# Attention loop: batch preparation of K and V spread over turns, first additions on GpSimd, router sums for five tiles at once

## The chip, the cores and the metric

The kernel runs on one core of a Trainium2 chip. A core has five engines with an instruction queue each, which meet only through semaphores: TensorE (PE in the profile; its weight loads are PEld), VectorE (DVE), ScalarE (ACT), GpSimd (POOL) and SyncE (SP), which here only issues transfers. Data lie in SBUF (128 partitions) and in PSUM, where TensorE writes its products. The metric is device time in microseconds (us), lower is better.

## The reference

Three stages follow each other. First, attention over pooled keys and values: 8 batches, 8 heads, 576 positions, head size 64; each run of 8 positions of K and V is averaged, so a batch has 72 keys per head. Then a mixture of 8 experts, each token in its best two by noisy logits. Last, a dense layer of width 2048.

```python
k_p = k.reshape(B, H, Sp, pool, D).mean(axis=3)      # pool = 8, Sp = 72
v_p = v.reshape(B, H, Sp, pool, D).mean(axis=3)
scores = scale * np.matmul(q, k_p.transpose(0, 1, 3, 2))
scores = scores - np.max(scores, axis=-1, keepdims=True)
attn = np.exp(scores)
attn = attn / (np.sum(attn, axis=-1, keepdims=True) + 1e-09)
x = np.matmul(attn, v_p)                             # then to (4608, 512)
...
logits = x @ w_gate
noise_scale = np.log1p(np.exp(x @ w_noise))
noisy_logits = logits + noise_scale * noise          # two best experts of each token
...
h = np.maximum(x[mask] @ w1[e], 0.0)
out[mask] += top2_w[mask, k, None] * (h @ w2[e])     # for each expert
...
h = x @ w_in
g = h - np.tanh(h)
return (g @ w_out).astype(np.float32)
```

## The kernel before

The 4608 tokens are 36 tiles of 128. A batch is 4.5 tiles, so batch b begins in tile T0 = floor(4.5 b): 0, 4, 9, 13, 18, 22, 27, 31. The attention loop has 42 turns (`for t in range(NT + 6)`), and a tile goes through it as through a pipeline. Turn t issues for different tiles, in this order on each engine:

- TensorE: small products of the batch preparation (`pe_step`), the transposes of the weights of attention of tile t-2 (`st_attT`, L1330), of q of tile t+2 (`st_q`, L1288), the scores of tile t+1 (`st_scores`, L1298), the product with the router's weights of tile t-5 (`st_x`, L1355, into the one buffer px), and attention times V of tile t-3 (`st_av`, L1342).
- VectorE: the reciprocal of the sums of tile t-1 (`st_norm`, L1316 and L1319), reading px of tile t-6 (`st_g`: xr L1364, lg L1367, and the sum lz L1368), the two maxima of the scores of tile t+1 (mx, L1301), and then the jobs of the turn (`at_step`).
- ScalarE: exponentials (L1312) and the copies out of PSUM (xT L1348, aT L1331, qT L1290, kb L1278).

All engines run their queues strictly in this written order (`manual_schedule`), so a VectorE job that is long makes the next turn's lg late; TensorE's next product L1355 needs px, which lg frees, and everything behind L1355 waits as well.

The batch preparation, for each b: K and V are loaded with the eight positions of a pool side by side in a row, and three additions halve them (`add` with n = 4, 2 and 1: 128x1280, 128x640 and 128x320 elements). For K the result is spread with a mask (`ke`, L1233), transposed by TensorE (L1276) and copied by ScalarE (L1278) into `KB[b % 2]`; this is `kb`, at the head of turn T0-2. For V a maximum (`vm`, L1243) goes over TensorE and VectorE to a power of two (`vt`: L1247 and L1250; `vs`: L1254, then L101 to L1269), and `vs` writes `VB[b % 2]` (L1260). Each batch has two buffers for its K and V: kt_109 and vt_111 for even b, kt_110 and vt_112 for odd b. The jobs stand at fixed turns:

```python
at(max(T0 - 4, 0), add, nc.vector, b, "k", 4)
at(max(T0 - 3, 1), P[b]["k"])
at(max(T0 - 2, 1), add, nc.vector, b, "v", 4)
at(max(T0 - 1, 2), P[b]["v"])
at_pe(T0 - (1 if b == 1 else 2), P[b]["kb"])
```

Into the same turns go the preparation of the first expert's weights (`Prep`: four loads, four `amax` of 128x1024, four `high` on ScalarE, four `low` of 128x1024 on VectorE, for w1 and then w2), and for each group of some ten tiles the router's jobs (`gate_jobs`, then `lists`): from the turn in which the group's last lz is there, `tick()` puts about seven of their small VectorE instructions into each turn, between those above. `lists` has two instructions of 128x800 (l_one, l_col) and five of 128x256 (l_row) for each five tiles. After the loop come the experts and the dense layer, in which TensorE is busy nearly without a gap.

Of the kernel before, what the change touches and what calls it, by code (L numbers as in the profile page):

```python
# [10 lines left out]
F32 = mybir.dt.float32  # L11
# [4 lines left out]
OP = mybir.AluOpType  # L16
AX = mybir.AxisListType
# [1092 lines left out]
def attention(nc, tc, st, V):  # L1110
    q, k, v, w_gate, w_noise, noise = (V[n] for n in ("q", "k", "v", "w_gate", "w_noise", "noise"))
    B, H, S, D, N, E, DM, SP, NT, HP = (V[n] for n in ("B", "H", "S", "D", "N", "E", "DM", "SP", "NT", "HP"))
# [113 lines left out]
    def prep_jobs(b, first=False):  # L1226
        tl = {}

        def kpool():
            add(nc.vector, b, "k", 2)  # L1230
            add(nc.vector, b, "k", 1)
            tl["ke"] = wk.tile([128, 5, 2, D], F32, name="ke", bufs=1)
            tt(tl["ke"], KV[b, "k"][:, :, 0:1].to_broadcast([128, 5, 2, D]), odd[:, :, :, None].to_broadcast([128, 5, 2, D]),  # L1233
               op=OP.mult)

        def vpool():
            add(nc.vector, b, "v", 2)
            add(nc.vector, b, "v", 1)
            tl["va"] = KV[b, "v"]

        def vmax():
            tl["vm"] = wk.tile([128, 1], F32, name="vm")
            nc.vector.tensor_reduce(tl["vm"], tl["va"][:, :, 0], axis=AX.XY, op=OP.max, apply_absolute_value=True)  # L1243

        def vmaxT():
            p = ps.tile([1, 128], F32, name="pt", bufs=4)
            nc.tensor.transpose(p, tl["vm"], identf)  # L1247
            yield
            tl["vx"] = wk.tile([1, 1], F32, name="vx")
            nc.vector.tensor_reduce(tl["vx"], p, axis=AX.X, op=OP.max)  # L1250

        def vscale():
            p = ps.tile([128, 1], F32, name="pt", bufs=4)
            nc.tensor.matmul(p, ones1, tl["vx"], start=True, stop=True)  # L1254
            yield
            m = wk.tile([128, 3], F32, name="vs")
            pow2(nc, m, p)
            of8 = wk.tile([128, 5, 4], F32, name="of8")
            ts(of8, of, m[:, 2:3], None, op0=OP.mult)
            tt(VB[b % 2].rearrange("p c (j d) -> p c j d", d=D), tl["va"][:, :, 0:1].to_broadcast([128, 5, 4, D]),  # L1260
               of8[:, :, :, None].to_broadcast([128, 5, 4, D]), op=OP.mult)
            lo, hi = b * S, b * S + S
            t0, t1 = lo // 128, -(-hi // 128)
            for t in range(t0, t1):
                o0, o1 = max(lo - 128 * t, 0), min(hi - 128 * t, 128)
                if o1 - o0 < 128:
                    ts(isc[o0:o1, t:t + 1], m[o0:o1, 1:2], 1.0 / 128, None, op0=OP.mult)
            f0, f1 = -(-lo // 128), hi // 128
            ts(isc[:, f0:f1], m[:, 1:2].to_broadcast([128, f1 - f0]), 1.0 / 128, None, op0=OP.mult)  # L1269

        def kbd():
            for i, (c0, c1) in enumerate(((0, 3), (3, 5))):
                w = cuts[c1] - cuts[c1 - 1]
                p = ps.tile([128, 4, 128], F32, name="pt", bufs=4)[:, 0:c1 - c0, 0:w]
                for c in range(c0, c1):
                    nc.tensor.transpose(p[:, c - c0], tl["ke"][:w, c].rearrange("p i d -> p (i d)"), identf[:w, :w])  # L1276
                o = KB[b % 2][:, cuts[c0]:cuts[c1]].rearrange("p (c n) -> p c n", n=w)
                nc.scalar.activation(o, p, AF.Copy, scale=1.0 / 512)  # L1278
            yield
        return dict(k=kpool, v=vpool, vm=vmax, vt=vmaxT, vs=vscale, kb=kbd)  # L1280

    QT, SC, AT, ATT, PV, XT, SM, RC = {}, {}, {}, {}, {}, {}, {}, {}

# [71 lines left out]
            nc.tensor.matmul(p[:, m, 0:128 + 4 * E], xT[:, m], wgn[:, m], start=True, stop=True)  # L1355

    PX = {}

    def st_g(t):
        p, rc = PX.pop(t), RC.pop(t)  # L1360
        xr = wk.tile([128, DM], F32, name="xr", bufs=3)
        r = rc.rearrange("p (m i) -> p m i", i=2)[:, :, :, None]
        h = lambda a, n: a.rearrange("p m (i n) -> p m i n", n=n)
        tt(xr.rearrange("p (m i n) -> p m i n", m=HP, i=2), h(p[:, :, 0:128], D), r.to_broadcast([128, HP, 2, D]), op=OP.mult)  # L1364
        nc.sync.dma_start(x_d[128 * t:128 * t + 128, :], xr)
        lg = wk.tile([128, HP, 2, 2 * E], F32, name="lg", bufs=1)
        tt(lg, h(p[:, :, 128:128 + 4 * E], 2 * E), r.to_broadcast([128, HP, 2, 2 * E]), op=OP.mult)  # L1367
        nc.vector.tensor_reduce(lz[:, t], lg.rearrange("p m i e -> p e (m i)"), axis=AX.X, op=OP.add)  # L1368

    def psum(shape):  # L1370
        return ps.tile(shape, F32, name="pt", bufs=4)
# [137 lines left out]
    def at_pe(t, f):  # L1509
        pe_step.setdefault(t, []).append(f)  # L1510
        assert len(pe_step[t]) < 3

    P = {0: prep_jobs(0)}
    st_q(0)
    P[0]["k"]()
# [6 lines left out]
    at(0, P[0]["v"])  # L1522
    at(0, P[0]["vm"])
    at_pe(1, P[0]["vt"])
    at_pe(2, P[0]["vs"])
    TB = {b: (b * S) // 128 for b in range(B)}
    for b in range(1, B):
        P[b] = prep_jobs(b)
        T0 = TB[b]
        d = 1 if b == 1 else 0  # L1530
        if b > 1:
            at(T0 - 8, load_kv, b, "k")
            at(T0 - 7, load_kv, b, "v")
# [38 lines left out]
    for f, t in ((c1.fin1, 8), (c1.fin2, 12), (c2.fin1, 30), (c2.fin2, 33)):  # L1572
        at_pe(t, f)
    for j in range(4):
        at(1 + j, c1.load, [j])
        at(3 + j, c1.amax, j)
        at((12, 14, 15, 16)[j], c1.high, j, nc.scalar)
        at((13, 15, 16, 18)[j], c1.low, j)
        at(18 + 2 * j, c2.load, [j])
        at((21, 24, 26, 29)[j], c2.amax, j)  # L1580
# [102 lines left out]
```

## Time and profile before

| what | value |
|---|---|
| median of 3 runs | 1862.28 us (1858.55 to 1862.8) |
| profiled execution, first to last instruction | 1863.0 us |
| TensorE busy | 1775.1 us (95%) |
| VectorE busy | 1315.9 us (71%) |
| ScalarE busy | 940.7 us (50%) |
| GpSimd busy | 205.7 us (11%) |
| mean granted TensorE clock | 0.986 |

The profiled execution has no other time than its span, which lies 0.7 us above the median and 0.2 us above the slowest of the three runs. Shares of the whole span say little of the attention loop, which takes its first 250 us and has its own limits: its turns have to be read one by one in the timelines of TensorE and VectorE. A timeline's row names in brackets the idle time ahead of an instruction and what ended it. The granted clock is a share of 2.4 GHz: 0.5 is 1.2 GHz.

### The profile page before, as it was taken

How to read it: one execution, taken by the hardware profiler on the slowest of the kernel's cores; microseconds unless marked ns; L12 is line 12 of the kernel's file. 1: busy time of each engine (PE TensorE's matmuls, PEld its weight loads, DVE VectorE, ACT ScalarE, POOL GpSimd, SP SyncE). 2: the span in 40 equal slices, each digit the busy share in tenths (PEclk: the TensorE clock that was granted, in tenths of full speed). 3: DMA queues.
4: the chain of work that ended last, by engine and by line, in shares of the span. 5: the costliest groups of instructions: out<-in, count | busy, mean ns of one | idle time of the engine just before them, and what ended most of it. 6: DMA issues, size and time to landing. Idle time of an engine off the chain costs nothing. (4 is left out here: it accounts for less than half of the span.)

```text
span 1863.0 us, 28938 instructions
## 1 busy us (share of the span) xinstructions
PE 1775.1 (95%) x10791; PEld 1083.6 (58%) x10792; DVE 1315.9 (71%) x2680; ACT 940.7 (50%) x2249; POOL 205.7 (11%) x198
## 2 busy tenths in 40 slices
PE   7898889999999999999999999999999999999998
PEld 5887884444445454544545454566666666666664
DVE  5788877667666667666666456687878778787875
ACT  5686652343434344343434245565656666666554
POOL 1000000311203021110101012110100101010000
PEclk8898999999999999999999999999999999999999
DMA  9657323354474545453464344531313323141200
GB/s 217 186 156 209 86 75 108 108 160 119 138 223 117 160 136 157 135 158 88 139 155 118 88 122 117 119 86 33 91 41 68 77 45 84 30 91 42 40 24 25
DMA packets 264158, 203.45 MB, mean 109 GB/s; under 512 B 188160, under 2 KB 208640, under 8 KB 264000
## 3 DMA queue, kind: packets, MB, share of 16 engines
q1 hardware_dynamic: 251840, 162.16, 32.2%
q0 software_dynamic: 11904, 38.81, 8.1%
q8 instruction: 88, 1.44, 0.3%
q14 instruction: 70, 0.57, 0.1%
q10 hardware_dynamic: 256, 0.46, 0.1%
HBM read 121.82 MB, written 45.74 MB: 90 GB/s over the span
## 5 line engine op out<-in xcount | busy, mean ns | idle before, releaser
L359 ACT ACTIVATE hT<-ph 128x512 f16<-128x512 f32 (+2 forms) x192 | 96.8, 504 | 429.4 <-PE ph L357 429.2
L355 PE MATMUL ph<-xTp,pair 128*128 128x384 f16 (+2 forms) x736 | 247.1, 336 | 16.1 <-DVE hT L360 5.5
L356 PE MATMUL ph<-xTp,pair 128*128 128x384 f16 (+2 forms) x736 | 246.9, 335 | 0.4 <-DVE xTp L336 0.4
L357 PE MATMUL ph<-xTp,pair 128*128 128x384 f16 (+2 forms) x736 | 246.6, 335 | 0.0
L360 DVE SCALAR_TENSOR_TENSOR hT<-ph,hT 128x512 f16<-128x512 f32 (+2 forms) x192 | 110.6, 576 | 164.0 <-ACT hT L359 163.7
L1042 PE MATMUL py<-wo,gT 128*128 128x512 f16 x576 | 218.3, 379 | 1.0 <-DVE gT L989 1.0
L377 PE MATMUL py<-pair,hT 128*128 128x512 f16 x576 | 218.6, 379 | 0.0
L378 PE MATMUL py<-pair,hT 128*128 128x512 f16 x576 | 218.6, 379 | 0.0
L379 PE MATMUL py<-pair,hT 128*128 128x512 f16 x576 | 218.4, 379 | 0.0
L1040 PE MATMUL py<-wo,gT 128*128 128x512 f16 x576 | 218.3, 379 | 0.0
L1041 PE MATMUL py<-wo,gT 128*128 128x512 f16 x576 | 218.3, 379 | 0.0
L899 PEld LDWEIGHTS <-wi 128*128 128x128 f16 x1536 | 150.2, 98 | 71.3 <-issue 14.6
L315 POOL DMA_INDIRECT xg<-x_d,idx x75 | 85.3, 1138 | 676.5 <-DVE xp L342 467.9
L713 POOL DMA_INDIRECT y<-y_d,ridx x64 | 66.7, 1042 | 538.5 <-DVE y L724 238.4
L355 PEld LDWEIGHTS <-pair 128*128 128x128 f16 x768 | 75.4, 98 | 85.8 <-issue 27.8
L356 PEld LDWEIGHTS <-pair 128*128 128x128 f16 x768 | 75.4, 98 | 64.1 <-issue 9.0
L357 PEld LDWEIGHTS <-pair 128*128 128x128 f16 x768 | 75.6, 98 | 58.2 <-issue 2.6
L999 ACT ACTIVATE th<-th,bias 128x512 f32<-128x512 f32 x144 | 102.5, 712 | 3.3 <-DVE th L997 3.3
L1000 DVE SCALAR_TENSOR_TENSOR th<-th,t 128x512 f32<-128x512 f32 x144 | 98.4, 683 | 1.4 <-ACT th L999 1.4
L989 DVE TENSOR_TENSOR gT<-th,gT 128x512 f16<-128x512 f32 x144 | 98.6, 685 | 0.2 <-ACT gT L988 0.2
L1312 ACT ACTIVATE at<-psc,mx 128x72 f32<-128x72 f32 x288 | 87.5, 332 | 19.1 <-DVE mx L1301 19.1
L1042 PEld LDWEIGHTS <-gT 128*128 128x128 f16 x576 | 56.4, 98 | 69.3 <-DVE gT L989 1.4
(303 smaller groups left out, 3461.6 us busy)
## 6 DMA issues: line engine op xcount, KB each, us to landing
stage<-in_moe_w SPq DMA_DIRECT2D x64, 512.0 KB, 6.5
y_d<-ys SPq DMA_DIRECT2D x82, 256.0 KB, 2.1
x_d<-xr SPq DMA_DIRECT2D x36, 256.0 KB, 2.2
out<-o SPq DMA_DIRECT2D x36, 256.0 KB, 2.0
qt<-in_q SPq DMA_DIRECT2D x32, 256.0 KB, 6.3
raw<-in_moe_w_in SPq DMA_DIRECT2D x32, 256.0 KB, 3.0
raw<-in_moe_w_out SPq DMA_DIRECT2D x32, 256.0 KB, 3.1
kt<-in_k SPq DMA_DIRECT2D x7, 768.0 KB, 6.9
```

What stands on the lines that cost most here:

```text
L355: nc.tensor.matmul(p[:, :nt], w[:, 0, m, s], x[:, 0, m, :nt], start=(m == 0), stop=False)
L356: nc.tensor.matmul(p[:, :nt], w[:, 0, m, s], x[:, 1, m, :nt], start=False, stop=False)
L357: nc.tensor.matmul(p[:, :nt], w[:, 1, m, s], x[:, 0, m, :nt], start=False, stop=(m == KD - 1))
L360: stt(h[:, 1, :nt], p[:, :nt], 0.0, h[:, 0, :nt], op0=OP.max, op1=OP.subtract)
L377: nc.tensor.matmul(p, h[:, 0, s], w[:, 0, f], start=(f == 0), stop=False)
L378: nc.tensor.matmul(p, h[:, 0, s], w[:, 1, f], start=False, stop=False)
L379: nc.tensor.matmul(p, h[:, 1, s], w[:, 0, f], start=False, stop=(f == KF - 1))
L899: nc.tensor.matmul(p, w[:, a, m], y[:, c, b, m], start=(start and m + x == 0), stop=(m == 1 and x == 2), skip_group_check=True)
L999: nc.scalar.activation(q, q, AF.Square, bias=bias[:, 2:3], scale=SP5)
L1040: nc.tensor.matmul(p, g[:, 0, s], wo[:, 0, f], start=(f == 0), stop=False)
L1041: nc.tensor.matmul(p, g[:, 0, s], wo[:, 1, f], start=False, stop=False)
L1042: nc.tensor.matmul(p, g[:, 1, s], wo[:, 0, f], start=False, stop=(f == KF - 1))
```

## The change

It does five things. The first additions (n = 4) of K and V of batches 2 to 7 go from VectorE, where each was one instruction of 128x1280, to GpSimd, as five of 128x256. The remaining steps of K and V become single jobs (`k2`, `k1` with ke, `v2`, `v1` with vm), for which a small planner picks, in a window of turns ahead of the batch, the turn with the least load on its own list (`load`, in ns); ke is there two turns or more ahead of `kb`. `vt` and `vs` come one turn later (for b above 1), and V's load one turn later. The loads of the first expert's w1 go from turns 1 to 4 to turns 5 to 8, and its `amax`, `high` and `low`, like those of w2, to later turns, by the planner too. And lz is summed once for five tiles (four at two places, two at the end) out of a larger lg, in place of once for each tile.

```diff
-        def kpool():
+        def k2():
             add(nc.vector, b, "k", 2)
+
+        def k1():
             add(nc.vector, b, "k", 1)
             tl["ke"] = wk.tile([128, 5, 2, D], F32, name="ke", bufs=1)
...
+    sums = (0, 5, 10, 15, 20, 25, 29, 34)
...
-        lg = wk.tile([128, HP, 2, 2 * E], F32, name="lg", bufs=1)
-        tt(lg, h(p[:, :, 128:128 + 4 * E], 2 * E), r.to_broadcast([128, HP, 2, 2 * E]), op=OP.mult)
-        nc.vector.tensor_reduce(lz[:, t], lg.rearrange("p m i e -> p e (m i)"), axis=AX.X, op=OP.add)
+        if t in sums:
+            LG[0] = wk.tile([128, 5, HP, 2, 2 * E], F32, name="lg", bufs=2)
+            LG[1] = t
+        lg, t0 = LG
+        tt(lg[:, t - t0], h(p[:, :, 128:128 + 4 * E], 2 * E), r.to_broadcast([128, HP, 2, 2 * E]), op=OP.mult)
+        if t + 1 in sums or t + 1 == NT:
+            nc.vector.tensor_reduce(lz[:, t0:t + 1], lg[:, 0:t + 1 - t0].rearrange("p t m i e -> p t e (m i)"),
+                                    axis=AX.X, op=OP.add)
...
+    def first(b, nm):
+        for c in each:
+            add(nc.gpsimd, b, nm, 4, slice(*c))
+
+    for t in range(15, 35):
+        fixed(t, 1300)
...
-            at(T0 - 7, load_kv, b, "v")
-        at(max(T0 - 4, 0), add, nc.vector, b, "k", 4)
-        at(max(T0 - 3, 1), P[b]["k"])
-        at(max(T0 - 2, 1), add, nc.vector, b, "v", 4)
-        at(max(T0 - 1, 2), P[b]["v"])
-        at_pe(T0 - (1 if b == 1 else 2), P[b]["kb"])
-        at(T0 - 1 + d, P[b]["vm"])
-        at_pe(T0 + d, P[b]["vt"])
-        at_pe(T0 + 1 + d, P[b]["vs"])
...
+            at(T0 - 6, load_kv, b, "v")
+            at(T0 - 6, first, b, "k")
+            at(T0 - 4, first, b, "v")
+            chain((640, T0 - 5, T0 - 4, job["k2"]), (960, T0 - 5, T0 - 4, job["k1"]))
+            chain((640, T0 - 3, T0 - 1, job["v2"]), (640, T0 - 3, T0 - 1, job["v1"]))
+            at_pe(T0 - 2, job["kb"])
+        at_pe(T0 + 1, job["vt"])
+        at_pe(T0 + 2, job["vs"])
+        fixed(T0 + 2, 2000)
...
+    chain(*((1024, 8 + j, 9 + j, lambda j=j: c1.amax(j)) for j in range(4)))
+    chain(*((1024, 17 + j, 18 + j, lambda j=j: c1.low(j)) for j in range(4)))
...
-        at(1 + j, c1.load, [j])
+        at(5 + j, c1.load, [j])
...
+    for ops in sorted(spread, key=lambda ops: ops[0][2]):
+        t = 0
+        for w, lo, hi, f in ops:
+            t = min(range(max(lo, t), hi + 1), key=lambda t: load.get(t, 0))
+            fixed(t, w)
+            at(t, f)
```

What this makes of the order is seen at three places. First VectorE, before: turn 10 ends and turn 11 begins, with the jobs of turn 10 between: `vs` of batch 2 (vs to isc), and after it the second and third addition of batch 3's K and its ke, which `kb` at the head of turn 11 needs.

```order
L1301 TENSOR_REDUCE mx<-psc 128x4 x2
L101 TENSOR_SCALAR vs<-pt 128x1
L102 TENSOR_SCALAR vs<-vs 128x1
L103 TENSOR_SCALAR vs<-vs 128x1
L1259 TENSOR_SCALAR of_980<-of,vs 128x20
L1260 TENSOR_TENSOR vb_155<-vt_111,of_980 128x1280
L1267 TENSOR_SCALAR isc<-vs 64x1
L1269 TENSOR_SCALAR isc<-vs 128x4
L1141 TENSOR_TENSOR kt_110<-kt_110 128x5x128
L1141 TENSOR_TENSOR kt_110<-kt_110 128x5x64
L1233 TENSOR_TENSOR ke<-kt_110,odd 128x640
L1316 TENSOR_SCALAR sm<-sm 128x8
```

VectorE, after: the same additions and ke of batch 3 (line numbers are a few higher), now among the jobs of turn 9.

```order
L1303 TENSOR_REDUCE mx<-psc 128x4 x2
L1141 TENSOR_TENSOR kt_110<-kt_110 128x5x128
L1141 TENSOR_TENSOR kt_110<-kt_110 128x5x64
L1235 TENSOR_TENSOR ke<-kt_110,odd 128x640
L1318 TENSOR_SCALAR sm<-sm 128x8
L1321 RECIPROCAL rc<-sm 128x8
L1368 TENSOR_TENSOR xr<-px,rc 128x512
L1374 TENSOR_TENSOR lg<-px,rc 128x128
```

They have moved ahead by a turn and a half, and `vs` of batch 2, now in turn 11, has no other job in its turn.

The second place is SP's queue in turns 1 to 4, before: kt_109 and vt_111 are K and V of batch 2, stage takes w1, qt the q of a tile.

```order
L1135 DMA kt_109<-in_k 128x3x512
L1135 DMA kt_109<-in_k 96x2x512
L118 DMA stage<-in_moe_w 128x1024
L1157 DMA qt<-in_q 128x8x64
L1135 DMA vt_111<-in_v 128x3x512
L1135 DMA vt_111<-in_v 96x2x512
L1542 DMA nz<-in_moe_noise 128x36x8
L118 DMA stage<-in_moe_w 128x1024
L1157 DMA qt<-in_q 128x8x64
L118 DMA stage<-in_moe_w 128x1024
L1157 DMA qt<-in_q 128x8x64
L118 DMA stage<-in_moe_w 128x1024
```

SP's queue, after, from the second half of the same K load on.

```order
L1135 DMA kt_109<-in_k 96x2x512
L1157 DMA qt<-in_q 128x8x64
L1574 DMA nz<-in_moe_noise 128x36x8
L1157 DMA qt<-in_q 128x8x64
L1135 DMA vt_111<-in_v 128x3x512
L1135 DMA vt_111<-in_v 96x2x512
L1157 DMA qt<-in_q 128x8x64 x2
L1135 DMA kt_110<-in_k 128x3x512
L1135 DMA kt_110<-in_k 96x2x512
L118 DMA stage<-in_moe_w 128x1024
```

Two q loads now stand ahead of batch 2's V, and the first load of w1 behind four.

The third place is VectorE in turns 20 and 21, before: behind the jobs of turn 20 (the last of them batch 5's first addition of V) come the end of the first group's router jobs (g_e, g_ov), the reading of px, and the first lists.

```order
L1141 TENSOR_TENSOR vt_112<-vt_112 128x5x256
L1438 TENSOR_TENSOR g_e<-g_e,g_hi 128x20
L1316 TENSOR_SCALAR sm<-sm 128x8
L1440 TENSOR_SCALAR g_ov<-g_hi 128x20
L1319 RECIPROCAL rc<-sm 128x8
L1441 TENSOR_TENSOR g_e<-g_e,g_ov 128x20
L1364 TENSOR_TENSOR xr<-px,rc 128x512
L1367 TENSOR_TENSOR lg<-px,rc 128x128
L1368 TENSOR_REDUCE lz<-lg 128x16
L1456 TENSOR_TENSOR l_one<-slot,g_e 128x800
L1457 TENSOR_TENSOR l_col<-l_one,head 128x10x80
L1301 TENSOR_REDUCE mx<-psc 128x4
```

VectorE, after, at the same place; vb and isc are the end of `vs` of batch 4.

```order
L1262 TENSOR_TENSOR vb_155<-vt_111,of_1803 128x1280
L1269 TENSOR_SCALAR isc<-vs 64x1
L1271 TENSOR_SCALAR isc<-vs 128x4
L1447 TENSOR_TENSOR g_e<-g_e,g_hi 128x20
L1318 TENSOR_SCALAR sm<-sm 128x8
L1449 TENSOR_SCALAR g_ov<-g_hi 128x20
L1321 RECIPROCAL rc<-sm 128x8
L1450 TENSOR_TENSOR g_e<-g_e,g_ov 128x20
L1368 TENSOR_TENSOR xr<-px,rc 128x512
L1374 TENSOR_TENSOR lg<-px,rc 128x128
L1465 TENSOR_TENSOR l_one<-slot,g_e 128x800
L1466 TENSOR_TENSOR l_col<-l_one,head 128x10x80
```

The addition has gone, and `vs`, which stood a turn earlier, has come in its place; the router's own instructions have not moved.

## Rows read from the trace of the kernel before

**Rows 1.** Windows: start:end, length, busy (count) per engine, clock, DMA share, GB/s.
```profile
53.00:248.60 195.60, 172.50 (x1367) 163.92 (x1367) 160.28 (x430) 135.48 (x592) 0.00 (x0) 0.95 0.53 145
89.70:93.70 4.00, 4.00 (x22) 3.97 (x23) 1.75 (x5) 2.14 (x6) 0.00 (x0) 0.59 0.24 83
107.30:112.50 5.20, 5.20 (x45) 5.06 (x44) 3.56 (x11) 4.61 (x18) 0.00 (x0) 1.00 0.38 120
49.00:53.00 4.00, 4.00 (x21) 4.00 (x20) 2.55 (x6) 2.93 (x17) 0.00 (x0) 0.57 1.16 311
```

**Rows 2.** TensorE's waits from 56 to 252 us: total, times, longest.
```profile
PE pt L1276 <- DVE sm L1316: 5.2, 2, 3.0
PE px L1355 <- DVE lg L1367: 4.7, 3, 3.4
PE pt L1276 <- DVE g_oh L1413: 3.2, 1, 3.2
PE pt L1276 <- DVE ke L1233: 3.0, 2, 2.5
PE pt L1288 <- ACT xT L1348: 1.7, 2, 1.4
PE pt L1247 <- DVE vm L1243: 1.6, 1, 1.6
```

**Rows 3.** TensorE's timeline: start, length, instructions [idle before <- releaser].
```profile
48.77 0.63 PE L1288 MATMUL pt<-identf,qt 128*128 128x128 f32 x4 [3.82 <-DMA qt<-in_q]
...
89.68 0.52 PE L1276 MATMUL pt<-identf,ke 128*128 128x128 f32 x3 [2.25 <-DVE sm L1316]
...
107.28 1.95 PE L1342 MATMUL pt<-aT,vb 128*128 128x128 f32 x16
...
112.58 1.95 PE L1342 MATMUL pt<-aT,vb 128*128 128x128 f32 x16
...
179.92 2.47 PE L1355 MATMUL px<-wgn,xT 128*128 128x160 f32 x8 [3.40 <-DVE lg L1367]
182.18 3.62 PE L1342 MATMUL pt<-aT,vb 128*128 128x128 f32 x16
```

**Rows 4.** VectorE's timeline, turn 10 and turns 20 to 22.
```profile
84.98 0.15 DVE L101 TENSOR_SCALAR vs<-pt 128x1 f32<-128x1 f32 x1
...
87.34 1.33 DVE L1141 TENSOR_TENSOR kt<-kt 128x640 f32<-128x640 f32 x2
88.71 0.82 DVE L1233 TENSOR_TENSOR ke<-kt,odd 128x640 f32<-128x640 f32 x1
...
152.12 0.46 DVE L1301 TENSOR_REDUCE mx<-psc 128x4 f32<-128x288 f32 x1 [2.28 <-PE psc L1298]
...
164.50 0.28 DVE L1367 TENSOR_TENSOR lg<-px,rc 128x128 f32<-128x128 f32 x1
```

**Rows 5.** What SP's queue waited for, 0 to 285 us: total, times, longest.
```profile
SPq L1135 <- DVE isc L1269: 9.8, 1, 9.8
```

**Rows 6.** Groups by form, 0 to 460 us: busy, mean ns | idle before.
```profile
L1141 DVE TENSOR_TENSOR kt<-kt 128x1280 f32<-128x1280 f32 x7 | 10.3, 1476 | 0.0
L1368 DVE TENSOR_REDUCE lz<-lg 128x16 f32<-128x128 f32 x36 | 13.4, 371 | 1.2
L127 DVE TENSOR_REDUCE am<-stage 128x1 f32<-128x1024 f32 x20 | 24.0, 1209 | 4.3 <-DMA stage<-in_moe_w 4.3
```

**Rows 7.** GpSimd's timeline in the expert stage.
```profile
359.95 2.15 POOL L255 TENSOR_TENSOR qs<-qs,qs 128x512 f32<-128x512 f32 x1
...
363.30 1.27 POOL L255 TENSOR_TENSOR qs<-qs,qs 128x512 f32<-128x512 f32 x1
```

**Rows 8.** VectorE's timeline at the same time.
```profile
355.72 1.27 DVE L159 SCALAR_TENSOR_TENSOR pair<-stage,wsc,pair 128x1024 f16<-128x1024 f32 x1
...
363.55 2.10 DVE L159 SCALAR_TENSOR_TENSOR pair<-stage,wsc,pair 128x1024 f16<-128x1024 f32 x1
```

**Rows 9.** DMA issues, from the profile page: KB each, us to landing.
```profile
kt<-in_k SPq DMA_DIRECT2D x7, 768.0 KB, 6.9
```

More of the change, by code (lines that the diff above doesn't have):

```diff
@@ L1234, in kpool, with v2, v1 @@
                op=OP.mult)
-        def vpool():
+        def v2():
             add(nc.vector, b, "v", 2)
+        def v1():
             add(nc.vector, b, "v", 1)
             tl["va"] = KV[b, "v"]
-        def vmax():
             tl["vm"] = wk.tile([128, 1], F32, name="vm")
@@ L1279, in kbd @@
             yield
-        return dict(k=kpool, v=vpool, vm=vmax, vt=vmaxT, vs=vscale, kb=kbd)
+        return dict(k2=k2, k1=k1, v2=v2, v1=v1, vt=vmaxT, vs=vscale, kb=kbd)
     QT, SC, AT, ATT, PV, XT, SM, RC = {}, {}, {}, {}, {}, {}, {}, {}
@@ L1357, in attention @@
     PX = {}
+    sums = (0, 5, 10, 15, 20, 25, 29, 34)
+    LG = [None, 0]
     def st_g(t):
@@ L1514, in attention @@
     st_q(0)
-    P[0]["k"]()
+    P[0]["k2"]()
+    P[0]["k1"]()
     both(P[0]["kb"]())
@@ L1521, in attention @@
         at(0, add, nc.vector, 0, "v", 4, slice(*c))
-    at(0, P[0]["v"])
-    at(0, P[0]["vm"])
+    at(0, P[0]["v2"])
+    at(0, P[0]["v1"])
     at_pe(1, P[0]["vt"])
@@ L1526, in attention, with fixed, chain @@
     TB = {b: (b * S) // 128 for b in range(B)}
+    load = {}
+    spread = []
+    def fixed(t, w):
+        load[t] = load.get(t, 0) + w
+    def chain(*ops):
+        spread.append(ops)
+    def first(b, nm):
[3 more added lines that the diff above has]
+        fixed(t, 1300)
     for b in range(1, B):
         P[b] = prep_jobs(b)
-        T0 = TB[b]
-        d = 1 if b == 1 else 0
-        if b > 1:
-            at(T0 - 8, load_kv, b, "k")
-            at(T0 - 7, load_kv, b, "v")
-        at(max(T0 - 4, 0), add, nc.vector, b, "k", 4)
-        at(max(T0 - 3, 1), P[b]["k"])
-        at(max(T0 - 2, 1), add, nc.vector, b, "v", 4)
-        at(max(T0 - 1, 2), P[b]["v"])
-        at_pe(T0 - (1 if b == 1 else 2), P[b]["kb"])
-        at(T0 - 1 + d, P[b]["vm"])
-        at_pe(T0 + d, P[b]["vt"])
-        at_pe(T0 + 1 + d, P[b]["vs"])
+        T0, job = TB[b], P[b]
+        if b == 1:
+            at(0, add, nc.vector, b, "k", 4)
+            at(1, job["k2"])
+            at(1, job["k1"])
+            at(2, add, nc.vector, b, "v", 4)
+            at(3, job["v2"])
+            at(3, job["v1"])
+            at_pe(3, job["kb"])
+        else:
+            at(T0 - 8, load_kv, b, "k")
+            at(T0 - 6, load_kv, b, "v")
[7 more added lines that the diff above has]
+        fixed(T0 + 2, 2000)
     at(2, lambda: nc.sync.dma_start(nz, noise.rearrange("(t p) e -> p t e", p=128)))
@@ L1571, in attention @@
     c1, c2 = V["first"] = [Prep(nc, V, ep, psum, 0, w) for w in (1, 2)]
-    for f, t in ((c1.fin1, 8), (c1.fin2, 12), (c2.fin1, 30), (c2.fin2, 33)):
+    for f, t in ((c1.fin1, 14), (c1.fin2, 16), (c2.fin1, 31), (c2.fin2, 33)):
         at_pe(t, f)
+    chain(*((1024, 8 + j, 9 + j, lambda j=j: c1.amax(j)) for j in range(4)))
+    chain(*((1024, 17 + j, 18 + j, lambda j=j: c1.low(j)) for j in range(4)))
+    chain(*((1024, 24 + j, 27 + j, lambda j=j: c2.amax(j)) for j in range(4)))
     for j in range(4):
-        at(1 + j, c1.load, [j])
[L1576 to L1580, printed above, removed]
+        at(5 + j, c1.load, [j])
+        at(16 + j, c1.high, j, nc.scalar)
+        at(22 + j, c2.load, [j])
         if j < 2:
```

## The prediction

> **What bounds the kernel now.** I read first a table of windows over the attention loop, then TensorE's waits there, then the timelines of TensorE and VectorE around the longest waits. In the 195.6 us from turn 6 to turn 34 TensorE is busy 172.5 and VectorE 160.3, at a mean granted clock of 0.95 [rows 1]: neither is full, so they wait for each other in turn. A turn without a wait takes 112.58 - 107.28 = 5.3 us from one product with V to the next [rows 3]. What lies above that is in TensorE's waits: 11.4 us (5.2 + 3.2 + 3.0) at L1276, the transposes of ke, 4.7 us at L1355 for px, and 1.6 us at L1247 for vm [rows 2]. All three are for VectorE, whose jobs stand in one queue with the reading of px.
>
> The wait at L1276 is seen in turn 10 to 11. VectorE begins `vs` at 84.98, the second addition of K at 87.34 and ke at 88.71 [rows 4]; TensorE has nothing to do for 2.25 us until 89.68 [rows 3]. The wait also costs afterwards: in the 4 us behind it the granted clock is 0.59, against 1.00 in an undisturbed turn [rows 1], so mostly the lower level, 1.2 GHz. That is (1 - 0.59) x 4.0 = 1.6 us more.
>
> **What goes.** My sum is made against the profiled span of 1863.0 us, which is 0.7 us above the median; I subtract the result from the median.
>
> - The waits for ke: in the new order ke stands two turns or more ahead of `kb` for every batch from 2 on, so 11.4 us go. Four of the five are long ones (3.0, 2.25, 3.2 and 2.5 us), each with its stretch at the low clock: 4 x 1.6 = 6.4 us go too. What is late next at that place is nothing of VectorE's: TensorE goes from the product with V straight into the transposes.
> - The wait for q in turn 5: 3.82 us for a DMA [rows 3], then 4 us at 0.57 [rows 1], 1.7 us. SP stood 9.8 us at batch 2's V load, waiting for `vs` of batch 0 to let go of the buffer [rows 5], and the q loads with w1's behind it came late into a stretch whose DMA share is 1.16 [rows 1]. Now two q loads go ahead of that V load, and w1's four loads of 512 KB go four turns later, into a loop whose mean share is 0.53. 5.5 us go. Those loads stand in front of q loads again, but two turns ahead of their use and with no blocked load before them.
> - The waits for px: 4.7 us, the longest 3.40 [rows 2, 3]. Behind that one the product L1355 takes 2.47 us and the product with V 3.62 against 1.95 [rows 3]; with half of 2.47 given back as well this is 2.9 us. I let 7.6 us go here and put what comes back into the next part.
> - The wait for vm, 1.6 us: vm is now done in turn T0-1 and its transpose comes at T0+1. It goes.
>
> Together 11.4 + 6.4 + 5.5 + 7.6 + 1.6 = 32.5 us.
>
> **What stays or comes.** The twelve additions of 128x1280 (1.48 us each [rows 6]) take 17.8 us off VectorE. The new sums of lz take five times the elements at once: at least 640/1024 of the 1.21 us of `amax`, 0.76, at most five times the old 0.37, 1.86 [rows 6]; I take 1.3, as the old 0.37 for only 128 elements speaks for a strided reading that costs more for each. Eight of these are 10 us against 13.4: 3 us less in all. They stand behind lg, where VectorE mostly waits for the scores, so in place or path they cost nothing, except where lists follow.
>
> At the lists it doesn't fit. From the first maximum of turn 20 (152.12) to the end of turn 22's lg (164.78) VectorE needs 12.7 us [rows 4]. In the new order an addition of 1.48 and a sum of 0.37 have left this piece [rows 6], `vs` has come (87.34 - 84.98 = 2.36 [rows 4]), and a `low` of 1.27 [rows 8] stands for an `amax` of 1.21: 13.3 us. Two turns of 5.3 leave 10.6, and TensorE's product comes some 0.3 us behind the maximum. So px waits 2.4 us in turn 22, and such a gap has cost clock: 2.9 us where L1355 and the product with V came behind it. 5.3 us stay. Three or four other turns (the second half of each list, and the second group's lists) are over 5.3 us by 0.4 to 1.6 with the same durations; I take 4 us, with ends 0 and 10, because VectorE's mean load falls from 160.3 to some 140 in a loop that would be about 174 long.
>
> GpSimd's additions: no row shows one of 128x256. One of 128x512 takes 1.27, or 2.15 us when it meets VectorE [rows 7], so a half-wide one lies between 0.6 and 2.15; I take 0.7, half of the undisturbed row and a little, 3.5 us for the five. They start when the load has landed, 6.9 us after its issue [rows 9], two turns and more ahead of `k2`: three turns of 5.3 less 6.9 are 9 us of cover, so even 1.8 each is hidden; beyond that `k2` would hold VectorE's whole queue, and so px, in twelve places. What they do to VectorE: a `low` begun at 363.55 beside GpSimd takes 2.10 in place of 1.27 us [rows 8], 0.83 lost. The Trainium skill (SBUF — State Buffer, Who interferes with whom) says that a VectorE instruction with two SBUF inputs and a GpSimd instruction that reads SBUF exclude each other, the second waiting until the first has ended. The trace agrees with it, since both sides of that meeting were longer by 0.8 to 0.9 us; by the rule alone each of the 60 additions could hold up such an instruction for its whole length, which I take up as a rival. Two meetings for each of the 12 calls, at half the 0.83, are 10 us on VectorE; most of that falls into its idle time, 35 us before and more now. I take 2 us on the path, with ends 0 and 10.
>
> ScalarE's four `high` go four turns later; 135.5 busy of 195.6 us [rows 1] hides them, but for waits like the 1.7 us for xT [rows 2], which I leave as they are. After turn 34 VectorE's router jobs bound the last turns; their instructions stay, and two long sums stand for six short ones: 0. The expert stage has the same instructions, and TensorE bounds it, so what the loop gains moves the end.
>
> Sum: 32.5 - 5.3 - 4 - 2 = 21.2 us less; 1862.3 - 21.2 = 1841 us.
>
> **Rivals.**
> - The router's turns stay full. From turn 15 on VectorE has the router's jobs besides, and the gaps only move from L1276 to L1355. Then what goes surely is what lies before: the waits for ke of batches 2 and 3 (2.5 + 2.25 + 2 x 1.6 = 8) and q (5.5), and of the remaining 19 us half; less the same 11.3, this is 11.7 us: 1850.5. For it speaks that the first lists get no lighter; against it that the three longest gaps there stand at ke and at a `vs` that now has another turn.
> - Nothing comes back: all 32.5 us go, and no new wait: 1830. For it VectorE's falling load, against it the 13.3 us at the lists.
> - Slower by the shared port. If each of the 60 additions holds a VectorE instruction for 1.27 us, VectorE has 160.3 - 17.8 - 3 + 76 = 215.7 us to do in the loop, 20 more than the loop is long: 1882. It decides from (195.6 - 139.5) / 60 = 0.94 us for each addition. Against it: 0.83 us was lost to a GpSimd instruction twice as wide.
> - No change at the end: the loop ends earlier, but its last turns wait for VectorE's index lists, and VectorE carries its late jobs there: 1857 to 1863. Against it: VectorE waits for TensorE several times between turns 31 and 35, so it has nothing to carry.
>
> **How the numbers follow.** Forecast 0.58, own range 1834 to 1849; full router turns 0.17; nothing comes back 0.12; no change 0.07; slower 0.06. A change of 0.3%, 5.6 us, is about what a measurement can tell here. The first three are faster by more: 0.87; same 0.07; slower 0.06. The range goes from 1829 to 1855: it leaves out the last two cases, the upper end of the second, and the lowest part of the third.
>
> **What would show it.** Right: no wait at L1276 above 0.5 us from batch 2 on, none for q in turn 5, twelve groups of five GpSimd additions ended before `k2` or `v2` needs them, and the loop's mean clock above 0.97. A px wait of 2 to 3 us in turn 22, and the sum of lz at 0.8 to 1.9 us. Wrong: a wait of `k2` for GpSimd, VectorE's instructions with two SBUF inputs lengthened by 0.5 us and more in most turns, q late again behind w1's loads in turns 8 to 11, or a last stretch between the loop and the first expert's product that is longer by what the loop has gained.

## The result, and the profile after

The changed kernel takes 1841.41 us (median of 4 runs, 1840.93 to 1844.06), the kernel before 1862.54 us on the same chip (4 runs, 1858.55 to 1864.93): a ratio of 0.9889, with a 95% interval of 0.9877 to 0.9900. That is 21.1 us less; forecast were 21.2, and the profiled spans (1863.0 and 1839.1 us) differ by 23.9.

The first view compares the whole front of the program, from 14 us to the first product of the experts, which begins at 281.99 us before and at 262.80 after. Windows, columns as in [rows 1], of the kernel before:

```profile
14.00:281.99 267.99, 227.10 (x1768) 212.32 (x1768) 209.77 (x560) 174.10 (x757) 3.95 (x4) 0.93 0.55 150
```

The kernel after: the front; the window of the first line of [rows 1], in which it now gets four turns further; and turns 6 to 34 alone, with the same 1367 matmuls as that line:

```profile
14.00:262.80 248.80, 218.32 (x1765) 203.96 (x1764) 197.91 (x520) 173.11 (x756) 49.95 (x64) 0.96 0.61 161
...
53.00:248.60 195.60, 180.01 (x1503) 171.13 (x1501) 159.22 (x431) 142.43 (x609) 37.82 (x49) 0.98 0.56 153
...
46.87:226.84 179.97, 165.06 (x1367) 156.69 (x1367) 150.83 (x398) 136.94 (x606) 38.51 (x50) 0.98 0.60 164
```

The front is 19.2 us shorter. TensorE's idle time in it falls from 267.99 - 227.10 = 40.9 to 30.5 us, its busy time for the same matmuls from 227.1 to 218.3 us, at a granted clock that rises from 0.93 to 0.96: 10.4 us of waits and 8.8 us of clock. Not all of this can be put down to the change, since 2.0 us are there already in turn 3, where TensorE waits for kb of batch 1. TensorE before:

```profile
36.77 0.66 PE L1288 MATMUL pt<-identf,qt 128*128 128x128 f32 x4 [1.09 <-ACT kb L1278]
```

TensorE after:

```profile
34.77 0.66 PE L1290 MATMUL pt<-identf,qt 128*128 128x128 f32 x4 [1.10 <-ACT kb L1280]
```

This place lies between 33.8 and 36.8 us in the fourteen profiles of this study, and at 33.8, 35.3 and 36.8 in three of them (replanned twice and `high` later, below) whose programs are the same up to there, so the start scatters by itself. From there on the front is 17.2 us shorter, 9.8 of waits and 7.4 of clock. The other 4.7 us between the two spans arise in the expert stage, whose instructions are the same: from the first expert product to the end it takes 1581.0 us before and 1576.3 after, and from 1574.6 to 1581.0 over the fourteen profiles (two profiles of one kernel, replanned below, have 1580.0 and 1577.3). With a single profile of the kernel before it isn't shown whether any of the 4.7 us belongs to the change.

TensorE's waits after, 14 to 262.7 us (total, times, longest), to be held against [rows 2]:

```profile
PE px L1357 <- DVE lg L1374: 15.0, 7, 4.3
PE pt L1249 <- DVE vm L1245: 4.1, 1, 4.1
PE pt L1290 <- ACT xT L1350: 2.8, 3, 1.3
PE pt L1256 <- DVE vx L1252: 1.2, 2, 0.7
PE pt L1290 <- ACT kb L1280: 1.1, 1, 1.1
PE px L1357 <- DVE g_ii L1420: 1.0, 1, 1.0
```

The transposes of ke (now L1278) don't appear any more, nor does q for a DMA. vm's 4.1 us is the first batch's, which stood there before too. What remains are the waits for px, and they have grown: between 53 and 248 us five for lg, 9.0 us, and one of 1.0, against three of 4.7 us. TensorE's timeline after, at the places of [rows 3]:

```profile
44.28 0.66 PE L1290 MATMUL pt<-identf,qt 128*128 128x128 f32 x4 [1.26 <-ACT xT L1350]
...
101.59 1.95 PE L1344 MATMUL pt<-aT,vb 128*128 128x128 f32 x16
103.38 0.66 PE L1278 MATMUL pt<-identf,ke 128*128 128x128 f32 x5
...
146.10 2.47 PE L1357 MATMUL px<-wgn,xT 128*128 128x160 f32 x8 [3.81 <-DVE lg L1374]
148.36 2.41 PE L1344 MATMUL pt<-aT,vb 128*128 128x128 f32 x16
...
224.56 2.47 PE L1357 MATMUL px<-wgn,xT 128*128 128x160 f32 x8 [2.50 <-DVE lg L1374]
226.82 4.16 PE L1344 MATMUL pt<-aT,vb 128*128 128x64 f32 x32
```

At 103.38 the product with V runs straight into the transposes of ke. At 44.28 q waits for ScalarE's xT where it had waited 3.82 us for its load. At 146.10 (turn 22) and 224.56 (turn 34) stand the two long waits that came back, with slower matmuls behind them.

### The profile page after: what moved, and what is told of

The parts are those of the page before. It is cut to its first block, busy times and chain, and to the rows that moved or that the text cites. A ratio compares the mean times of both kernels' runs of the same rounds, so it can differ in the third digit from the quotient of the medians.

```text
span 1839.1 us, 28995 instructions
## 1 busy us (share of the span) xinstructions
PE 1763.2 (96%) x10791; PEld 1074.6 (58%) x10792; DVE 1304.3 (71%) x2640; ACT 940.1 (51%) x2249; POOL 251.4 (14%) x258
```

## The experiments

The runs were made on several chips, each beside the kernel before on the same chip, whose median was 1861.8 to 1865.0 us there. So runs are best compared by what they gain on it; the changed kernel gained 21.1 us.

### Only the additions of K moved

In the kernel before, one edit: K's VectorE jobs one turn earlier.

```diff
-        at(max(T0 - 4, 0), add, nc.vector, b, "k", 4)
-        at(max(T0 - 3, 1), P[b]["k"])
+        at(max(T0 - 5, 0), add, nc.vector, b, "k", 4)
+        at(T0 - 4 if b > 1 else 1, P[b]["k"])
```

> The kernel before, with one edit: for batches 2 to 7 the K jobs (first addition; second and third with ke) stand one turn earlier, all still on VectorE. Theory (order): the 11.4 us of waits at the transposes of ke and the 6.4 us of low clock behind them go; as VectorE's load is the same, about a third comes back as waits for px: 1850 us (1846 to 1854). Rival (load): the gaps only move to px: 1858 us or more.

1852.28 us against 1863.97 of the kernel before (0.9934, 0.9918 to 0.9951): 11.7 us of the 21 come from this edit, within the theory's 1846 to 1854. TensorE's waits, 14 to 260 us:

```profile
PE px L1355 <- DVE lg L1367: 10.7, 7, 4.1
PE pt L1247 <- DVE vm L1243: 5.7, 2, 4.1
PE pt L1288 <- DMA qt<-in_q: 3.6, 1, 3.6
```

No row of L1276 is left. The 11.4 us that stood there are gone with their clock. In exchange px's waits have grown by 4.3 us (10.7 less the 1.7 of a wait that belongs to the tail, against 4.7): VectorE still has the same work in its full turns.

### The first additions back on VectorE

In the changed kernel, the five GpSimd additions of each load become one of 128x1280 on VectorE again.

```diff
-        for c in each:
-            add(nc.gpsimd, b, nm, 4, slice(*c))
+        add(nc.vector, b, nm, 4)
```

> The changed kernel, with the first additions of K and V of batches 2 to 7 back on VectorE as twelve instructions of 128x1280, in the turns in which GpSimd had them (T0-6 and T0-4). Theory (order: the gain is that ke no longer stands behind vs in the last turn before its transposes): no wait for ke comes back, the 17.8 us of VectorE fall mostly into its idle time, and some 5 us (2 to 8) come back as waits for px in the router's turns: 1846 us. Rival (load: the gain is what GpSimd took off VectorE): most of the 17.8 us come back: 1856 us or more. Rival (shared port: GpSimd costs VectorE as much as it takes off): 1841 us or less.

1848.95 us against 1863.97 (0.9920, 0.9904 to 0.9937): 15.0 us of gain in place of 21.1, so the move to GpSimd is worth some 6 us, within the theory's 2 to 8 and under a third of the whole. There is no wait for ke; two new px waits (1.19 at 91.18 and 0.78 at 187.73) come with the additions, and the one of turn 22 is 4.13. The front of this profile is 6.3 us longer than that of the changed kernel, but 3.3 of these are TensorE's clock after turn 34, which comes and goes with no known reason (last section); the 6 us rest on the times.

This run also prices the port. From 14 us to the first expert product VectorE is busy 204.42 us here and 197.91 with the additions on GpSimd: 6.5 us less, where twelve times 1.48 are 17.8. So up to 11.3 us went into other VectorE instructions that became longer. Added up over the groups by form, where stretches in which two overlap count twice, they are 9.3 us longer: 0.16 to 0.19 for each of the 60 additions. The groups by form, of this kernel:

```profile
L1470 DVE TENSOR_TENSOR l_row<-slot,g_row 128x256 f16<-128x256 f16 x25 | 9.9, 414 | 0.0
L1318 DVE TENSOR_SCALAR sm<-sm 128x8 f32<-128x8 f32 x36 | 5.8, 162 | 0.0
```

And of the changed kernel, with its sums of lz:

```profile
L1470 DVE TENSOR_TENSOR l_row<-slot,g_row 128x256 f16<-128x256 f16 x25 | 11.5, 476 | 0.0
L1318 DVE TENSOR_SCALAR sm<-sm 128x8 f32<-128x8 f32 x36 | 8.4, 233 | 0.0
L1376 DVE TENSOR_REDUCE lz<-lg 128x80 f32<-128x640 f32 x6 | 7.5, 1254 | 0.2
```

The largest share, 2.6 us, falls on sm, an instruction of 128x8 with one tensor as input, and the next, 1.6 us, on l_row.

### vt and vs one turn earlier again

In the changed kernel, with V's load left late:

```diff
-        at_pe(T0 + 1, job["vt"])
-        at_pe(T0 + 2, job["vs"])
+        d = 1 if b == 1 else 0
+        at_pe(T0 + d, job["vt"])
+        at_pe(T0 + 1 + d, job["vs"])
```

> The changed kernel, with vt and vs of batches 2 to 7 one turn earlier again, as before the change. Theory (order of ke): ke stays early, so no wait at its transposes; vs falls into fuller turns (turn 23 with lists, turn 19 with two low) and px waits grow by some 4 us: 1845 us. Rival (what freed ke was the move of vs, not the move of ke): waits at the transposes of ke come back for three batches or more, with low clock behind them: 1850 us or more.

1850.42 us (0.9930, 0.9914 to 0.9947): 13.6 us of gain in place of 21.1, and neither theory had the whole reason. The rival's waits for ke are absent. The theory's growth at px is absent too: the loop's px waits sum to 10.0 us, as in the changed kernel, and have only moved. On TensorE's timeline the first row is a new wait, for vm, and the second the longest px wait, now in turn 24:

```profile
148.91 0.27 PE L1249 MATMUL pt<-identf,vm 128*1 128x128 f32 x1 [2.54 <-DVE vm L1245]
...
167.51 2.47 PE L1357 MATMUL px<-wgn,xT 128*128 128x160 f32 x8 [4.85 <-DVE lg L1374]
```

vm isn't ready when its transpose is first in TensorE's queue, three times (4.8 us in all), since V's last additions may stand as late as turn T0-1; and in turn 23 vs stands among the lists, with batch 6's ke behind it (the planner still counts vs one turn later). So the later vt is no by-product: it is what makes the planner's window for V safe. How much of the 7.6 us this is stays open: the profiled execution was the fastest of the four (1847.28 us), and its front is only 3.7 us longer than that of the changed kernel.

### What had made q late: the order in SP's queue

Three runs of the changed kernel, with w1's loads early again, with V's load early again, and with both:

```diff
-        at(5 + j, c1.load, [j])
+        at(1 + j, c1.load, [j])
...
-            at(T0 - 6, load_kv, b, "v")
+            at(T0 - 7, load_kv, b, "v")
```

> The changed kernel with w1's four loads issued four turns earlier again, in turns 1 to 4, as before the change; V's loads stay one turn later. Theory (q came late in turn 5 because SP stood blocked at V's load and only then issued q's load; w1's traffic alone is not enough): no wait of TensorE's transposes of q for a DMA above 1 us, time 1840 to 1843. Rival (the traffic of w1's four loads of 512 KB in front of q's is what made it late): q waits 2.5 to 4 us for a DMA in turns 4 to 6, the clock falls behind it, and the time is 1845 to 1847 (3.8 us and 1.7 us of clock).

> The changed kernel with each V load issued one turn earlier again, in turn T0-7 as before the change, so that for batch 2 it stands in SP's queue ahead of the q loads and waits there until vs of batch 0 lets go of the buffer; w1's loads stay late. Theory (the blocked load is the cause of the late q): SP stands some 5 to 15 us at that load in turn 1, q waits 2 to 4 us for a DMA in one of the turns 3 to 5, time 1844 to 1847. Rival (w1's traffic is the cause, and without it a blocked load does no harm): SP is blocked as well, but q's wait stays under 1 us and the time is 1840 to 1843. If both this kernel and the one with w1 early show no such wait, only both together make it.

> The changed kernel with both of the edits of the runs v_early and w1_early together: V's loads one turn earlier and w1's four loads four turns earlier, so that SP's queue is ordered around q as before the change. Alone, the early V load made q wait 2.16 us in turn 4 to 5, and the early w1 loads made none. Theory (the blocked V load holds q back, and w1's loads issued in front of the late q add to it): q waits 3.5 to 4.2 us for a DMA, as the 3.82 us before the change, the clock falls behind it, and the time is 1844 to 1848. Rival (w1's loads play no part): q waits 2.2 us as in v_early, and the time is v_early's, 1842 to 1845.

Measured were 1842.69 us with w1 early (0.9880, 0.9857 to 0.9903), 1843.71 with V early (0.9890, 0.9868 to 0.9912) and 1843.84 with both (0.9898, 0.9882 to 0.9915). The three intervals overlap with the changed kernel's, so the waits decide, not the times. With w1 early q never waits for a DMA. TensorE with V early:

```profile
PE pt L1290 <- DMA qt<-in_q: 2.2, 1, 2.2
```

TensorE with both early:

```profile
PE pt L1290 <- DMA qt<-in_q: 3.4, 1, 3.4
```

SP's queue with both early, up to 60 us:

```profile
SPq L1135 <- DVE isc L1271: 9.3, 1, 9.3
```

The blocked V load is the cause, and w1's loads, which alone make no wait, make it longer when q is already late (2.2 to 3.4 us, one profile each): the third run's theory in kind, a little short of its 3.5 to 4.2. The price is smaller than I had put it. In both of the kernels in which q waits for its load, the 1.26 us for xT at 44.28 is absent: with q in time, TensorE stands at the same place for ScalarE. Net the order of SP's queue is worth some 2.5 us by the medians, not 5.5: 18.7 us of gain with both early, against 21.1 and, for the changed kernel measured again below, 21.3. That lies within the intervals.

### lz summed for each tile

```diff
-    sums = (0, 5, 10, 15, 20, 25, 29, 34)
+    sums = tuple(range(NT))
```

> The changed kernel with one edit taken back: the logits' exponentials are summed for each tile (36 sums of 128 elements at 0.37 us) in place of 8 sums over up to five tiles. Theory (these sums stand behind the reading of the logits, where VectorE waits for TensorE anyway): the time stays within 2 us of the changed kernel's 1841.4, VectorE is busy some 3 us longer, and px's waits in the loop sum to 9.5 us give or take 2, as in the changed kernel. Rival (VectorE's load decides, whatever the job): 3 to 5 us slower, 1844.5 to 1846.5, with px waits longer by as much.

1840.56 us (0.9879, 0.9859 to 0.9898), no slower than the changed kernel. VectorE is busy 201.72 us up to the first expert product in place of 197.91, and px's waits in the loop are 9.6 us. The sums for five tiles save 3.8 us of VectorE that TensorE doesn't wait for. In the tail they even cost something: px's last wait is 3.41 us here and 4.29 in the changed kernel, where a sum of 1.24 us stands ahead of the last group's lists.

### Twice the additions on GpSimd

```diff
         for c in each:
             add(nc.gpsimd, b, nm, 4, slice(*c))
+        for c in each:
+            nc.gpsimd.tensor_add(junk, junk, junk)
```

> The changed kernel with each of the twelve calls of five GpSimd additions of 128x256 followed by five more of the same shape on a scratch tile, whose result nobody uses: 120 additions in place of 60. Theory (the shared port costs path only where a VectorE instruction meets an addition; 2 us per 60): 1841 to 1847, best guess 1843.5; VectorE's instructions with two SBUF inputs are lengthened only where they overlap, and px's waits in the loop grow by no more than 3 us. Rival (each addition holds a VectorE instruction for its own length, 0.69 us): 60 more are 41 us of VectorE's time in a loop with some 35 us of slack, 1850 or more. Second rival (no cost at all): within 0.5 us of the changed kernel in the same profile stretch, px's waits the same.

1847.98 us (0.9912, 0.9893 to 0.9931): 17.0 us of gain, 4.1 less than the changed kernel and 4.3 to 7.4 less than the three kernels above with V early, w1 early and lz for each tile, which ran on the same chip. So sixty more additions cost some 4 to 7 us: at the upper end of the theory's range or a little above it, less than the rival's, and far from none. Here `junk` is a scratch tile. VectorE is busy 205.9 us up to the first expert product, 8.0 more, 0.13 for each added addition. Where the path pays is seen at one place. GpSimd's timeline:

```profile
115.87 4.82 POOL L1141 TENSOR_TENSOR vt<-vt 128x256 f32<-128x256 f32 x5 [7.08 <-DMA vt<-in_v]
120.66 3.37 POOL L1550 TENSOR_TENSOR junk<-junk 128x256 f32<-128x256 f32 x5
```

VectorE's timeline at the same time:

```profile
120.02 0.77 DVE L1413 TENSOR_TENSOR g_nl<-g_p,lz 128x80 f32<-128x80 f32 x1
120.71 0.57 DVE L1318 TENSOR_SCALAR sm<-sm 128x8 f32<-128x8 f32 x1
...
121.46 0.59 DVE L1419 TENSOR_TENSOR g_ii<-g_nl,tops 128x80 f32<-128x80 f32 x1
```

TensorE's:

```profile
122.99 1.40 PE L1357 MATMUL px<-wgn,xT 128*128 128x160 f32 x8 [2.23 <-DVE lg L1374]
124.19 3.54 PE L1344 MATMUL pt<-aT,vb 128*128 128x128 f32 x16
```

Three small VectorE instructions that take 0.17 to 0.24 us at this place in the changed kernel take 0.57 to 0.77 here; lg comes late, px waits 2.23 us where the changed kernel waits 0.99, and the product with V behind it takes 3.54 in place of 1.95 us. Of the rest of this profile's delay 3.3 us are TensorE's clock at turn 34 (below) and 1.9 us the start; its own time, 1854.0 us, is 6 us above the median of its runs.

### The planner's loads taken from the trace

In the changed kernel the planner counts 1.3 us for each of the turns 15 to 34. Here it gets for each turn what VectorE spent there on the router and lists in the trace. The first expert's scaling and `high` come earlier, and `low` is kept out of turns 20 and 21; the K jobs of batches 5 and 6 and the V jobs of batch 5 are pinned to turns 19, 22 and 18; and the last batch's vs stands a turn earlier, out of turn 33 with its lists.

```diff
-    for t in range(15, 35):
-        fixed(t, 1300)
+    for t, n in zip(range(15, 35), (300, 1700, 400, 1500, 600, 2600, 4200, 600, 3700, 200,
+                                    300, 700, 1700, 1700, 800, 1200, 3800, 600, 3700, 2000)):
+        fixed(t, n)
+    KW, VW = {5: (19, 19), 6: (22, 22)}, {5: (18, 18)}
...
-    chain(*((1024, 17 + j, 18 + j, lambda j=j: c1.low(j)) for j in range(4)))
+    chain(*((1200, t, t, lambda j=j: c1.low(j)) for j, t in enumerate((16, 17, 19, 22))))
...
-        at(16 + j, c1.high, j, nc.scalar)
+        at(14 + j, c1.high, j, nc.scalar)
```

> The changed kernel, with the planner's load list filled from the router's jobs as the trace shows them (3.7 to 4.2 us in the turns with lists, 0.2 to 1.7 us else), batch 5's V jobs pinned to turn 18, K jobs of batches 5 and 6 to turns 19 and 22, the w1 scaling two turns earlier with low in turns 16, 17, 19 and 22, and batch 7's vs in turn 32. Theory (what is left in the loop is VectorE's jobs piled up beside the lists): the px waits of 3.8, 1.75 and 2.5 us in turns 22, 24 and 34 shrink to 1 us or less each and with them the low clock: 7 to 9 us less than the changed kernel, 1833 us. Rival (VectorE's load as a whole bounds the router's turns, so waits only move): within 3 us of the changed kernel, 1838 to 1844 us.

1839.48 us (0.9871, 0.9855 to 0.9888): the rival's time, though the front is 7.8 us shorter, as the theory had it. Two windows, the front and the one in which the changed kernel's clock was 0.98:

```profile
14.00:255.00 241.00, 214.83 (x1761) 200.41 (x1760) 193.10 (x520) 173.22 (x756) 48.81 (x64) 0.97 0.63 167
53.00:248.60 195.60, 178.60 (x1517) 169.46 (x1516) 163.82 (x448) 143.28 (x610) 38.38 (x49) 1.00 0.56 155
```

Both long px waits have gone, and the clock is full (1.00) in the second window. VectorE is busy 193.1 us up to the first expert product, against 197.9. To see whether the gain reaches the end I ran the changed kernel and this one again on one chip, with a third in which the first halves of w1 on ScalarE come a turn later:

```diff
-        at(14 + j, c1.high, j, nc.scalar)
+        at(15 + j, c1.high, j, nc.scalar)
```

> The changed kernel itself, run beside the two below so that they can be compared with it on one chip, and profiled a second time. Theory (the same wait of 2.50 us for px in turn 34 is followed by a low clock of changing length: the next product with V took 4.16 us in one profile, 6.9 in others): 1840 to 1844; px waits at the same places with the same lengths within 0.1 us, while the step from that wait to the next long one takes either about 25.1 or about 28.4 us. Rival (the scatter of the profiles comes from waits of another length): the waits themselves differ by 1 us and more between the two profiles.

> The kernel of the earlier run named replanned (the planner's loads taken from the trace, so that no px wait of 2.5 and 3.8 us stands in turns 22 and 34), again, beside the changed kernel. Theory (what the loop gains moves the end): its loop was 7.8 us shorter in the profile and its time 5 to 8 us below the changed kernel's, 1834 to 1837. Rival (the loop's gain is lost again in the expert stage, whose profile took 1580.0 us where the changed kernel's took 1576.3): 1838 to 1841, 1 to 3 us below the changed kernel, and the expert stage again some 3 us longer.

> The replanned kernel with one edit: ScalarE's four first halves of w1 (high, 1.15 us each) go one turn later, from turn 15 on. In replanned the first of them stood in ScalarE's queue in turn 14 and waited 1.6 us for the scale, with the exponentials of that turn behind it, and TensorE waited 1.6 us for xT in turn 15 and lost some 3 us by turn 17. Theory: no wait for xT above 1.1 us in turns 14 to 16, the loop 2 to 3 us shorter than replanned's, the time 2 to 3 us below it in the same comparison. Rival (the wait only moves to the next high): the loop and the time are those of replanned within 1 us.

Against 1861.79 us before (11 runs), the changed kernel took 1840.46 us (6 runs, 1836.64 to 1844.14; 0.9890, 0.9870 to 0.9909), the replanned one 1836.32 (6 runs, 1831.46 to 1841.72; 0.9866, 0.9844 to 0.9888) and the one with `high` later 1835.52 (5 runs, 1832.16 to 1838.48; 0.9860, 0.9840 to 0.9880). So some 4 to 5 us of the gain reach the end. The 7.8 us of the first profile were too many: in this second pair of profiles the front is 4.7 us shorter (258.57 against 263.27). And the first of the replanned runs had gained 24.5 us on the kernel before of its own chip, 3.4 more than the changed kernel. The intervals of the ratios overlap, but five of the six runs of the changed kernel are slower than all five with `high` later; 0.8 us between the two replanned kernels is nothing. `high` later takes away the 1.6 us for xT in turn 15, but 1.45 us for xT come at 108.02: there the rival was right.

## Why the prediction came out right, point by point

- **What bounds the loop** was read rightly: px, ke and vm, all for VectorE. From turn 3 on the front lost 9.8 us of waits and 7.4 of clock, 17.2 in all; the prediction's terms, sorted in the same way, are 21.5 - 8.4 = 13.1 us of waits and 11.0 - 2.9 = 8.1 of clock.
- **The waits for ke** (17.8 us with their clock): none is left, and this part alone gives 11.7 us net of what comes back at px.
- **The wait for q** (5.5): cause right, a V load that blocks SP, but the size is about half by the runs (2.5), and by the traces 3.82 - 1.26 + 1.7 = 4.3. I had not asked of this wait what is late next: xT is, 1.26 us at the same place.
- **The px waits** are the term that was sized worst. 2.4 us forecast in turn 22 are 3.81; turns 24 and 34, two of the "three or four other turns", have 1.75 and 2.50. In the loop 10.0 us of px waits and 1.6 + 1.6 of clock came, 13.2, against 5.3 + 4 + 2 = 11.3, within the ends. The reason given held: from the first maximum of turn 20 to the end of turn 22's lg VectorE takes 15.0 us, where 13.3 were forecast and two turns are 10.6. Its timeline from the first maximum of turn 21 on:

```profile
138.47 0.45 DVE L1303 TENSOR_REDUCE mx<-psc 128x4 f32<-128x288 f32 x1
...
140.20 1.28 DVE L159 SCALAR_TENSOR_TENSOR pair<-stage,wsc,pair 128x1024 f16<-128x1024 f32 x1
141.40 1.34 DVE L1141 TENSOR_TENSOR vt<-vt 128x640 f32<-128x640 f32 x2
...
143.18 0.97 DVE L1470 TENSOR_TENSOR l_row<-slot,g_row 128x256 f16<-128x256 f16 x1
144.07 0.69 DVE L1318 TENSOR_SCALAR sm<-sm 128x8 f32<-128x8 f32 x1
...
145.68 0.27 DVE L1374 TENSOR_TENSOR lg<-px,rc 128x128 f32<-128x128 f32 x1
```

  GpSimd's at the same time:

```profile
143.15 3.88 POOL L1141 TENSOR_TENSOR vt<-vt 128x256 f32<-128x256 f32 x5 [10.19 <-DMA vt<-in_v]
```

  `low`, V's last additions and the lists stand in one turn, and two instructions at its end (0.97 for l_row in place of 0.41, 0.69 for sm in place of 0.16) meet these five additions: 1.1 us of what the forecast was short. Two in turn 20, g_hi and g_row, meet the five that GpSimd begins at 129.40 (0.35 and 0.66 us, 0.17 and 0.18 before), which is 0.7 more.
- **The additions on GpSimd**: 17.8 us off VectorE and 10 back by lengthening were forecast, 9.3 to 11.3 measured. A call of five takes 3.47 us where nothing meets it, as forecast, 5.20 at most, and all twelve had ended before `k2` or `v2` came. The 2 us for the path are likely too little: sixty more cost some 4 to 7 us, and the first sixty may have cost as much. No run here has the additions without such meetings, so this stays open. One reading of [rows 7] and [rows 8] was wrong, without harm to the sum: the 2.15 us on GpSimd and the 2.10 on VectorE are not two sides of one meeting. At 359.95 GpSimd came second, behind a `low` that VectorE had begun at 358.97; at 363.55 VectorE came second, behind GpSimd's addition of 363.30, which took its 1.27. Only the second was held up each time.
- **The sums of lz** (1.3 us each, 3 in all, none on the path): 1.25 us, 3.8 and none in the loop. Of the eight sums six are over five tiles, one over four and one over two.
- **ScalarE's `high`** (0): they go three or four turns later, and the waits of q's transposes for xT in the loop are 1.6 us, 1.7 before.
- **The tail** (0): the product with V of turn 35 comes 21.3 us earlier, the first expert product 19.2. Of these 2 us 0.9 is the longer last px wait (4.29 against 3.41), for the long lz sum ahead of the last lists, and 1.2 is the product behind it (2.47 us in place of 1.32). This term, put at nothing, was missing from the sum.

That the sum agrees with the medians to 0.1 us is luck: the ratio's interval is 2 us wide on either side, and from turn 3 to the first expert product the profiles differ by 17.2 us, not 21.2; the start and the expert stage, of which the sum has nothing, gave the rest. In waits the forecast 13.1 lose 1.3 at q (1.26 for xT), 1.6 at px (10.0 against 8.4) and 0.9 in the tail, which leaves 9.3 where 9.8 were measured; the rest is in small waits. The rival of full router turns (1850.5) was right in that px's waits grow there, but the waits for ke went there too, all of them, and with them the clock. The slower rival is far off: at most 0.19 us for each addition, where it decides from 0.94.

## What to carry to other kernels

When a wait on a strictly ordered queue is removed, look first at which other engine's result the same instruction needs next, and when that comes: the second wait is what remains of the first. A planner that spreads jobs by load is as good as its loads; with the per-turn times of the trace in place of one constant, and the jobs moved that these showed in full turns, some 4 us more were to be had here, by the medians. Moving work to GpSimd paid here, where it emptied the queue that bounds the loop, some 6 us. It would be better put into turns in which VectorE waits, which no run here tried, since beside it even an instruction of 128x8 took four times its length (0.69 us in place of 0.16).

## What the runs showed of the hardware

The short sm was not expected. VectorE's sm at 91.14 lies within GpSimd's additions of 89.81 to 93.85 and takes 0.69 us, the length of one addition, in place of 0.16:

```profile
91.14 0.69 DVE L1318 TENSOR_SCALAR sm<-sm 128x8 f32<-128x8 f32 x1
```

GpSimd's timeline at the same time:

```profile
89.81 4.04 POOL L1141 TENSOR_TENSOR vt<-vt 128x256 f32<-128x256 f32 x5 [9.01 <-DVE mx L1303]
```

The Trainium skill (SBUF — State Buffer, Who interferes with whom) names tensor_scalar, besides instructions with two inputs in SBUF, among those that can take the port pair shared with GpSimd, when its operands let it run in a two-port mode, and says that whoever comes second waits for the whole instruction. The trace agrees with it in the length, 0.69 us; in which mode sm runs no trace shows. The prediction had counted only instructions with two inputs. The reciprocal of the same tile, right behind sm at 91.86 and within the same additions, takes its usual 0.20 us.

The same gap does not always cost the same clock. px's wait of 2.50 us in turn 34 stands with this length in eight profiles. From its end to the end of the next long px wait it takes 25.06 us in the changed kernel, and 25.1 to 25.5 in its second profile, with lz summed for each tile and with both loads early; in the four others (additions on VectorE, w1 early, V early, additions twice) it takes 28.38 to 28.40. TensorE with w1 early, against the 4.16 us above for the same 32 matmuls:

```profile
221.57 2.05 PE L1357 MATMUL px<-wgn,xT 128*128 128x160 f32 x8 [2.50 <-DVE lg L1374]
223.41 6.93 PE L1344 MATMUL pt<-aT,vb 128*128 128x64 f32 x32
```

In the kernel before, with no wait in turn 34, these 32 matmuls take 3.68 us and the product with px ahead of them 1.32, so the gap cost about 1.6 us of clock in four executions and, with the 3.3 us between the two steps, about 5 in four others. What decides between them no run here shows; that a single profile can be 3.3 us off by this alone is the reason why small edits were judged by their waits.
